# Sparse attention and a routed expert layer on one core: head pairs written in one hand order, with half-array scores, row copies by DMA and the last unit's sums on GpSimd

## The chip, the cores and the metric

The kernel runs on one core of a Trainium2 chip. A core has a TensorE (PE: matrix multiplications into PSUM), a VectorE (DVE), a ScalarE (ACT), a GpSimd (POOL, which also issues the indirect DMAs and the weight loads) and a SyncE (SP, which only issues DMAs). Each works through its own queue of instructions in order, and semaphores tie the queues together. The metric is the device time of one execution in microseconds (us); of several executions the median is compared.

## The reference

There are 4 batches of 8 heads, 768 tokens, 64 elements per head. Keys are cut into 24 chunks of 32. For each query an upper bound of its product with each chunk is computed from the chunk's minimum and maximum; the six best chunks that are not in the future are kept, and causal attention runs over those alone:

```python
ub = np.sum(np.maximum(q * k_min, q * k_max), axis=-1)   # per query and chunk
top_chunks = np.argsort(np.where(causal, ub, -1e9), axis=-1)[..., -6:]
scores = np.where(sel & (pos_q >= pos_k), (q @ k.T) / 8, -1e9)
x = softmax(scores) @ v                  # rows of 8 heads x 64 = 512
logits = x @ w_gate                      # 8 experts
out[token] = prob(best expert) * (relu(x @ w1[e]) @ w2[e])
```

The second part is a top-1 expert layer over the 3072 tokens: each token goes through one of 8 experts (512 to 1024 to 512) and is scaled by the gate's probability.

## The kernel before

**Head pairs.** Attention works on 16 pairs of heads, i = 0 to 15, four per batch (`hp` is the pair's place in its batch). For each pair, Q, K and V are loaded as 128 tokens by (6 blocks, 2 heads, 64). Several steps for different pairs run at the same time:

- *Preparation* (`prep_steps`, L191 to L268). TensorE turns K and Q by transposes (L202, L212), three 128-column blocks at a time. VectorE takes each chunk's maximum and minimum (L204, L205) and copies Q in f32 (`qT`, L219); ScalarE takes |Q| (`qA`, L220) and writes the bf16 operands: both heads' halves of K into `KTE` (L206, L207), the second head's half of Q into `QSB` (L222). GpSimd writes the first head's half of Q (L221). `kse` puts sums and differences of maxima and minima into `KS` and `KD` (L229, L230).
- *Selection*. `ub` multiplies `KS` with Q and `KD` with |Q| (L236), both heads and both halves of the queries in 64-row blocks; `select` turns the result (L244), adds a causal bias (L247), finds the eight largest per row (L252) and marks what lies below the sixth (L255). `mask` turns the marks (L262) and ScalarE writes them into rows 64 and up of `QSB` (L264, L265), where they meet rows of -50 in `KTE`, so that the score matmul adds the mask.
- *Attention*. Seven units u = 0 to 6 per pair: units 0 and 1 are the first 384 queries, 2 to 6 the second. `scores` is a bf16 matmul of 128 keys by up to 384 queries per head (L291), an exp on ScalarE (L296) into a tile `P`, and causal masks on GpSimd for the diagonal blocks (L300): units 0, 1 (twice), 5, 6 (twice). `attend` multiplies V with `P` in f32, each head on half of the array's columns (L313), copies the output when it is complete (`ot`, L318), and adds the unit's `P` to a running sum `acc` on VectorE (L325), which later gives the denominators.
- *Router* (`router_steps`, `route_steps`). `ud` takes denominators and gate products for the pair on 32-column pieces of the array (L341, L346); `lgp` turns them and divides (L354 to L358); `xr` turns the outputs, scales them and writes the token rows (L377, L379). Once per batch `logits`, `rank` and `scatter` choose experts and send the rows to DRAM in expert order.

**Order.** TensorE, GpSimd and SyncE follow the program's order. In the pairs, VectorE and ScalarE are ordered by the framework's planner; only the first pair and the last pair with the experts are by hand for them too. A pair is cut in four groups g (L722 to L771): units (0, 1), (2, 3), (4, 5), (6), and around them the steps of pairs i - 1, i + 1 and i + 2, with the scores 0 and 1 of pair i + 1 in the last group. Weights come in 32 pieces (`load_w`), spread over the groups on GpSimd's queue.

**Array shape.** A matmul uses the whole 128x128 array, or 64 or 32 of its columns, by the width of its stationary operand. Scores and transposes of f32 tiles use all of it; attend, `ub` and the mask's transposes 64; `ud` 32.

**Buffers.** PSUM has 8 banks: three in `ps_m` (preparation, selection, router), two of two banks each in `ps_s` (scores), one in `ps_o` (attend's output).

**Experts.** 28 tiles of 128 tokens are gathered (L542), turned by DMA (L554), and go through `up` (L589, Relu at L592, turned by DMA at L593) and `down` (L600, scaled at L607, scattered at L608).

Of the kernel before, what the change touches and what calls it, by code (L numbers as in the profile page):

```python
# [12 lines left out]
I32 = mybir.dt.int32  # L13
# [11 lines left out]
def kernel(  # L25
# [52 lines left out]
    cbias = const.tile([128, 3, 2, NCH], FP32)  # L78
    thr = const.tile([128, NT], FP32)
# [26 lines left out]
    def consts_first():  # L106
# [3 lines left out]
        colc = work.tile([128, S], BF16, tag="Pr", bufs=4, name="colc")  # L110
# [11 lines left out]
        nc.gpsimd.memset(nsel[:], 0.0)  # L122

    def consts_bias():
# [4 lines left out]
        for t in range(NT):  # L129
            nc.vector.tensor_scalar(thr[:, t:t + 1], chunk_p[:], float(4 * t), None, ALU.add)  # L130
# [4 lines left out]
    def consts_last():  # L135
        nc.gpsimd.memset(KS[1][:], 0.0)
        nc.gpsimd.memset(KD[1][:], 0.0)
        nc.gpsimd.memset(QSB[1][64:128], 0.0)
        nc.gpsimd.tensor_copy(out=KTE[1][64:128], in_=KTE[0][64:128])
# [18 lines left out]
    def load_w(s_):  # L158
# [7 lines left out]
        nc.gpsimd.dma_start(out=dst, in_=src.rearrange("(c p) f -> p c f", p=128))  # L166

    late, sums_ = [], []

    def flush(*qs):  # L170
        for q_ in qs or (sums_, late):
            for f_ in q_:
                f_()
            q_.clear()
# [5 lines left out]
    def load(i, *names, eng=nc.sync):  # L180
        b, hp = divmod(i, HP)
        for nm, src in (("k", k), ("q", q), ("v", v)):
            if nm not in names:
                continue
            t_ = ld.tile([128, NT, 2, D], FP32, tag=nm, bufs=2 if nm == "v" else 1)
            for hd in range(2):
                eng.dma_start(out=t_[:, :, hd, :],
                                  in_=src[b, 2 * hp + hd].rearrange("(t p) d -> p t d", p=128))
            st[i][nm] = t_

    def prep_steps(i):  # L191
        s = st[i]
        kte, qsb, ks, kd = KTE[i % 2], QSB[i % 2], KS[i % 2], KD[i % 2]
        kmx = {}

        def k_half(hf):
            if hf == 0:
                s["kmx"] = work.tile([128, NCH], FP32, tag="kmx", name="kmx")
                s["kmn"] = work.tile([128, NCH], FP32, tag="kmn", name="kmn")
            pt = ps_m.tile([128, 384], FP32, tag="m")  # L200
            for t in range(3):
                nc.tensor.transpose(pt[:, ts(t, 128)], s["k"][:, 3 * hf + t], ident_f[:])  # L202
            pk = pt[:].rearrange("p (c w) -> p c w", w=CH)
            nc.vector.tensor_reduce(s["kmx"][:, ts(hf, 12)], pk, AX.X, ALU.max)  # L204
            nc.vector.tensor_reduce(s["kmn"][:, ts(hf, 12)], pk, AX.X, ALU.min)  # L205
            nc.scalar.activation(kte[0:64, 0, ts(hf, 384)], pt[0:64, :], AF.Copy, bias=0.0, scale=0.125)  # L206
            nc.scalar.activation(kte[0:64, 1, ts(hf, 384)], pt[64:128, :], AF.Copy, bias=0.0, scale=0.125)  # L207

        def q_t(hf):
            pt = ps_m.tile([128, 384], FP32, tag="m")  # L210
            for t in range(3):
                nc.tensor.transpose(pt[:, ts(t, 128)], s["q"][:, 3 * hf + t], ident_f[:])  # L212
            s[f"qp{hf}"] = pt

        def q_e(hf):
            pt = s[f"qp{hf}"]
            qT = work.tile([128, 384], FP32, tag=f"qT{hf}")
            qA = work.tile([128, 384], FP32, tag=f"qA{hf}")
# [13 lines left out]
        def ub():  # L232
            pu = ps_m.tile([128, 384], FP32, tag="m")
            for w_, nm in ((ks, "qT"), (kd, "qA")):
                for hf in range(2):
                    nc.tensor.matmul(pu[64 * hf:64 * hf + 64, :], lhsT=w_[:], rhs=s[f"{nm}{hf}"][:],  # L236
                                     start=(nm == "qT"), stop=(nm == "qA"), skip_group_check=True)
# [626 lines left out]
```

## Time and profile before

| what | value |
|---|---|
| median of 3 runs | 364.26 us (364.17 to 366.05) |
| the profiled execution's own time | 363.95 us |
| its span, first to last instruction | 362.1 us |
| TensorE busy | 335.4 us, 93% |
| ScalarE busy | 235.2 us, 65% |
| VectorE busy | 232.1 us, 64% |
| GpSimd busy | 177.1 us, 49% |
| first scores | 16.7 us |
| denominators of pair 0, of pair 13 | 41.89 and 231.90 us |
| first `up`, last matmul of `down` | 248.8 and about 352.5 us |

All values but the first row come from one profiled execution. In a line of a group of instructions stand the source line, the engine, the operation, what is written and read, the shape, how often, then busy time and the mean duration of one; in a line of the timeline, the start, the length and the same names. For a matmul the words before the element shape are the array's rows and columns in use. An f32 matmul leaves two records. Matmuls overlap in the pipeline, so the distance between starts says more than a duration.

### The profile page before, as it was taken

To read this page: it belongs to the slowest core of one execution; us is meant where nothing else is said; L and a number is where in the kernel's file an instruction comes from. 1 tells how busy PE (TensorE), PEld (TensorE's weight loads), DVE (VectorE), ACT (ScalarE), POOL (GpSimd) and SP (SyncE) were. 2 spreads that over 40 slices of the span, in tenths; PEclk is the share of its full clock that TensorE was granted. 3 is DMA by queue.
4 is the path that set the end of the run, shared out by engine and by line. 5 is a ranking of instruction groups with operands and counts; after the bars stand their busy time and mean duration, and the time that the engine had idled before them with its cause. 6 is when DMAs were issued, how large, how long until landed. Compare 5 with 4: busy or idle time off the path is not lost. (4 is left out here: it accounts for less than half of the span.)

```text
span 362.1 us, 7547 instructions
## 1 busy us (share of the span) xinstructions
PE 335.4 (93%) x2312; PEld 173.4 (48%) x2312; DVE 232.1 (64%) x811; ACT 235.2 (65%) x398; POOL 177.1 (49%) x296
## 2 busy tenths in 40 slices
PE   6777999999999999999999997998999899999990
PEld 5534455465554554554545544443544344444440
DVE  5789788898998898998988999775370010000000
ACT  2496797797887977977879778462354445544450
POOL 3074333452476343457424538375576765555331
PEclk9999999999999999999999998999999999999996
DMA  7619997999948989957989992366999999999841
GB/s 148 114 24 198 201 206 113 217 194 177 219 108 185 191 121 195 205 123 193 167 138 201 183 186 67 83 125 121 164 193 236 204 245 211 215 197 193 175 123 51
DMA packets 138215, 59.83 MB, mean 165 GB/s; under 512 B 122811, under 2 KB 131005, under 8 KB 138176
## 3 DMA queue, kind: packets, MB, share of 16 engines
q1 hardware_dynamic: 119072, 29.52, 45.9%
q0 software_dynamic: 17536, 29.42, 42.0%
q10 hardware_dynamic: 1568, 0.39, 0.6%
q8 instruction: 21, 0.34, 0.4%
q14 instruction: 18, 0.15, 0.1%
HBM read 56.14 MB, written 10.51 MB: 184 GB/s over the span
## 5 line engine op out<-in xcount | busy, mean ns | idle before, releaser
L325 DVE TENSOR_TENSOR Pa<-Pa,Pr 128x768 f32<-128x768 f32 (+2 forms) x112 | 81.5, 728 | 1.8 <-DVE Pa L325 0.5
L300 POOL TENSOR_SCALAR_AFFINE_SELECT Pr<-Pr 128x256 f32<-128x256 f32 x80 | 31.9, 418 | 76.2 <-ACT Pr L296 75.3
L296 ACT ACTIVATE Pr<-ps 128x768 f32<-128x768 f32 (+2 forms) x112 | 65.0, 628 | 3.2 <-PE ps L291 2.9
L600 PE MATMUL py<-w_all,hT 128*128 x224 | 52.6, 379 | 1.0 <-DMA hT<-h__4066 0.8
L291 PE MATMUL ps<-QSB,KTE 128*128 128x384 bf16 (+2 forms) x288 | 49.1, 294 | 1.7 <-ACT QSB L265 1.2
L542 POOL DMA_INDIRECT xg<-xs_dram,grow x28 | 29.9, 1068 | 22.6 <-DVE gt_all L565 7.4
L563 DVE TENSOR_TENSOR ti_all<-xg,inv_i 128x1 int32<-128x1 int32 x17 | 2.8, 163 | 58.0 <-DMA xg<-xs_dram,grow 58.0
L291 PEld LDWEIGHTS <-KTE 128*128 128x128 bf16 x288 | 24.2, 98 | 32.6 <-issue 25.3
L608 POOL DMA_INDIRECT out_dram<-y,ti_all x28 | 27.8, 994 | 24.4 <-ACT y L607 18.7
L600 PEld LDWEIGHTS <-hT 128*128 128x128 bf16 x224 | 21.8, 98 | 27.6 <-DMA hT<-h__4066 1.2
L607 ACT ACTIVATE y<-py,gt_all 128x512 f32<-128x512 f32 x27 | 18.5, 687 | 20.6 <-PE py L600 19.9
L349 ACT ACTIVATE ud<-pu 128x384 f32<-128x384 f32 x16 | 7.9, 492 | 36.5 <-PE pu L346 36.5
L443 POOL DMA_INDIRECT xs_dram<-xrow,sli x24 | 26.9, 1121 | 6.6 <-issue 4.5
L589 PE MATMUL ph<-w_all,KTE 128*128 x120 | 28.4, 379 | 0.0
L296 ACT ACTIVATE Pa<-ps 128x768 f32<-128x768 f32 x32 | 26.0, 813 | 2.9 <-PE ps L291 2.3
L166 POOL DMA_DIRECT2D w_all<-in_moe_w_dram x32 | 24.4, 762 | 0.0
L300 POOL TENSOR_SCALAR_AFFINE_SELECT Pa<-Pa 128x256 f32<-128x256 f32 x16 | 6.5, 405 | 36.5 <-ACT Pa L296 36.5
L589 PE MATMUL ph<-w_all,QSB 128*128 x96 | 22.7, 379 | 0.2 <-issue 0.2
L379 DVE TENSOR_TENSOR xrow<-pt,rec 128x384 bf16<-128x384 f32 x32 | 17.6, 552 | 3.0 <-PE pu L236 1.7
L204 DVE TENSOR_REDUCE kmx<-pt 128x12 f32<-128x384 f32 x30 | 16.7, 556 | 4.0 <-PE pt L202 3.9
L221 POOL CAST QSB<-qT 64x384 bf16<-64x384 f32 x30 | 16.7, 564 | 4.1 <-DVE qT L219 2.7
L318 DVE COPY ot<-po 128x384 f32<-128x384 f32 x32 | 17.7, 553 | 1.2 <-PE po L313 1.2
(306 smaller groups left out, 639.5 us busy)
## 6 DMA issues: line engine op xcount, KB each, us to landing
w_all<-in_moe_w_dram POOLq DMA_DIRECT2D x32, 512.0 KB, 6.0
xg<-xs_dram,grow POOLq DMA_INDIRECT x28, 3.9
out_dram<-y,ti_all POOLq DMA_INDIRECT x28, 4.3
t__122<-in_k_dram SPq DMA_DIRECT2D x2, 192.0 KB, 3.5
t__125<-in_q_dram ACTq DMA_DIRECT2D x2, 192.0 KB, 4.0
t__128<-in_v_dram SPq DMA_DIRECT2D x2, 192.0 KB, 5.6
t__196<-in_k_dram SPq DMA_DIRECT2D x2, 192.0 KB
t__206<-in_q_dram SPq DMA_DIRECT2D x2, 192.0 KB, 3.7
```

Of the source, the lines that this page charges most:

```text
L166: nc.gpsimd.dma_start(out=dst, in_=src.rearrange("(c p) f -> p c f", p=128))
L291: nc.tensor.matmul(pv[:, hd, :], lhsT=kte[:, hd, ts(kb, 128)], rhs=qsb[:, hd, ds(qb * 384 + 384 - w, w)], start=True, stop=True, skip_grou ...
L296: nc.scalar.activation(P[:, :, ds(c0, w)], pv, AF.Exp)
L300: nc.gpsimd.affine_select(out=pd, in_=pd, pattern=[[0, 2], [1, 128]], compare_op=ALU.is_ge, fill=0.0, base=0, channel_multiplier=-1)
L318: nc.vector.tensor_copy(out=ot[:], in_=po[:])
L325: nc.vector.tensor_tensor(acc[:, :, 384 - w:384], acc[:, :, 384 - w:384], P[:, :, ds(c0, w)], ALU.add)
L443: d = nc.gpsimd.indirect_dma_start(out=xs_dram[:], out_offset=bass.IndirectOffsetOnAxis(ap=sli[:, u:u + 1], axis=0), in_=bst[b][f"xrow{u % ...
L542: d = nc.gpsimd.indirect_dma_start(out=xg_bufs[j % XB][:].bitcast(I32), out_offset=None, in_=xs_dram[:], in_offset=bass.IndirectOffsetOnAx ...
L589: nc.tensor.matmul(ph[:, fh, :], lhsT=xT[:, c, :], rhs=w_all[:, ds(wo + (c * F + fh * 512), 512)], start=(c == 0), stop=(c == NDC - 1), sk ...
L600: nc.tensor.matmul(py[:], lhsT=hT[:, c, :], rhs=w_all[:, ds(wo + (W1W + c * DM), DM)], start=(c == 0), stop=(c == NFC - 1))
L607: nc.scalar.activation(y[:], py[:], AF.Copy, bias=0.0, scale=fs[j]["gt"])
L608: d = nc.gpsimd.indirect_dma_start(out=out[:], out_offset=bass.IndirectOffsetOnAxis(ap=fs[j]["ti"], axis=0), in_=y[:], in_offset=None, bou ...
```

## The change

- **One order for all engines.** All five queues follow one written order, `iteration(i)`, for every pair; the planner orders nothing in the pairs any more. `prep_steps`, `scores` and `attend` are cut into smaller steps (matmul, evacuation, sum), so that each can be placed alone.
- **Two visits of the full array.** Within a pair, everything that needs all 128 columns stands in two places: Q's and the selection's transposes with scores 2 and 3; and scores 6 with K's, the gate's and the output's transposes. Scores 0, 1, 4 and 5 are computed as two halves of 64 keys each (`split=True`), on 64 columns of the array (not units 0 and 1 of pair 0).
- **Rows by DMA.** K and Q are written once in bf16 for both heads (`kB` by ScalarE, `qB` by GpSimd), and `rows` copies each head's 64 rows into `KTE` and `QSB` with two DMAs on SyncE.
- **Sums on GpSimd.** The two additions of unit 6 run on GpSimd behind that unit's masks. The second output of a pair is copied by ScalarE instead of VectorE.
- **Less of the first block.** The first 128 queries need no selection; the bounds, the bias and the mask cover 640 queries in 2 x 320 columns (`c0s`, `cbase`).
- **Exp in one piece.** Units 1 and 6 place their two parts side by side, and one exp covers both.
- **PSUM.** The output of the first half comes from `ps_m`, K's transposes from `ps_s`. `Pr` has three buffers instead of four.
- **First pair.** K and Q are loaded with one head on each of two queues, V later; the mask is computed twice into two banks, which ScalarE and VectorE empty at the same time.
- **Weights.** Half of the pieces (`w2`) are laid out so that a partition takes four rows in a row; Relu reads its PSUM tile with a stride so that `h` matches.
- **Router and table.** Logits stand early in a batch's second pair, and the early expert table is built in one piece in pair 14.

```diff
+    def k_red(i, hf):
+        pk = s["pk"][hf].rearrange("p (c w) -> p c w", w=CH)
+        for nm, op in (("kmx", ALU.max), ("kmn", ALU.min)):
+            d = nc.vector.tensor_reduce(s[nm][:, ts(hf, 12)], pk, AX.X, op)
...
+    def k_ev(i, hf):
+        d = nc.scalar.activation(st[i]["kB"][:, ts(hf, 384)], st[i]["pk"][hf], AF.Copy, bias=0.0, scale=0.125)
...
+    def rows(i, nm, dst):
+        for hd in range(2):
+            nc.sync.dma_start(out=dst[i % 2][0:64, hd, :], in_=st[i][nm][64 * hd:64 * hd + 64, :])
...
+    def q_c(i):
+        for hf in range(2):
+            nc.gpsimd.tensor_copy(out=st[i]["qB"][:, ts(hf, 384)], in_=st[i]["qT"][:, hf])
...
+                nc.tensor.matmul(pu[64 * h:64 * h + 64, 0:320], lhsT=w_[i % 2][:],
+                                 rhs=x_[:, ds(128 + 320 * h, 320)],
...
+    def s_mm(i, u, split=False):
+        for kb, w, c0 in parts:
+            for hd in range(2):
+                for h in range(2 if split else 1):
+                    n = 64 if split else 128
+                    nc.tensor.matmul(ps[ds(h * n, n), hd, ds(c0, w)], lhsT=kte[:, hd, ds(kb * 128 + h * n, n)],
+                                     rhs=qsb[:, hd, ds(qb * 384 + 384 - w, w)],
...
+    def add(i, u):
+        for kb, w, c0 in parts:
+            (nc.gpsimd if u == 6 else nc.vector).tensor_tensor(acc[:, :, 384 - w:384], acc[:, :, 384 - w:384], P[:, :, ds(c0, w)], ALU.add)
...
-            nc.scalar.activation(h_[:], ph[:], AF.Relu)
+            nc.scalar.activation(h_[:].rearrange("q a (c p) -> q a c p", c=4),
+                                 ph[:].rearrange("q a (p c) -> q a c p", c=4), AF.Relu)
...
+    def iteration(i):
+        p, n, m = i - 1, i + 1, i + 2
+        for u in (0, 1):
+            s_mm(i, u, i > 0)
+            s_ex(i, u)
+        if i > 1:
+            rout[i - 2]["sums"]()
...
+            av(p, 6)
+            if not last:
+                load(n, "v")
+            o_ev(p, 1)
+            if router:
+                route[b - 1][0]()
+            if n < NP:
+                ub_mm(n)
+                ub_ev(n)
+            if m < NP:
+                q_prep(m)
+            if n < NP:
+                sel_mm(n)
+                sel_v(n)
...
+        for u in (2, 3):
+            s_mm(i, u)
+            s_ex(i, u)
...
+        pieces(i, 2)
+        av(i, 0)
+        av(i, 1)
+        add(i, 1)
+        o_ev(i, 0)
...
+        for u in (4, 5):
+            s_mm(i, u, True)
+            s_ex(i, u)
+        if 0 < i and m < NP:
+            q_c(m)
+        pieces(i, 1)
...
+        av(i, 2)
+        av(i, 3)
+        add(i, 3)
+        add(i, 4)
...
+            mask_ev(n, mask_mm(n))
+        if i > 0:
+            rt["ud_mm"]()
+            rt["ud_ev"]()
+        s_mm(i, 6)
+        if m < NP:
+            rows(m, "qB", QSB)
+        s_ex(i, 6)
...
+        add(i, 5)
+        add(i, 6)
...
+        if m < NP:
+            k_prep(m, True)
+            rows(m, "kB", KTE)
+            kse(m)
+        if i > 0:
+            rt["lgp_mm"]()
+            rt["lgp_v"]()
...
+            av(i, 4)
+        av(i, 5)
```

## The prediction

> **What bounds the kernel now.** I read the page first: engine shares, then the 40 slices.
>
> ```profile
> span 362.1 us, 7547 instructions
> ...
> PE 335.4 (93%) x2312; PEld 173.4 (48%) x2312; DVE 232.1 (64%) x811; ACT 235.2 (65%) x398; POOL 177.1 (49%) x296
> ...
> PE   6777999999999999999999997998999899999990
> ...
> DVE  5789788898998898998988999775370010000000
> ```
>
> TensorE is busy from slice 5 to slice 39, so it looks like the bound of attention and of the experts; VectorE is close behind, but only in the attention slices. A busy share can hide waits, so next I asked for the engines' busy time in one head pair, and then for TensorE's order of time in the same stretch.
>
> ```profile
> 131.40:145.60 14.20, 14.12 (x110) 7.57 (x109) 12.59 (x39) 11.65 (x22) 6.15 (x14) 1.00 1.08 182
> ```
>
> (Columns: length; busy time of PE, PEld, DVE, ACT, POOL; clock; DMA share; GB/s.) The first matmul of the denominators (L341) comes back every 14.19 us, pair after pair, so 14.2 us is the pitch.
>
> ```profile
> 133.40 0.82 PE L212 MATMUL pt<-ident_f,t__1831 128*128 128x128 f32 x6
> 134.15 0.87 PE L313 MATMUL po<-Pr,t__1683 128*64 128x256 f32 x8
> 134.95 0.82 PE L291 MATMUL ps<-QSB,KTE 128*128 128x384 bf16 x4
> ...
> 136.24 0.87 PE L313 MATMUL po<-Pa,t__1888 128*64 128x384 f32 x4
> 136.93 0.82 PE L313 MATMUL po<-Pr,t__1888 128*64 128x256 f32 x8
> 137.58 0.81 PE L236 MATMUL pu<-qT,KS 128*64 128x384 f32 x4
> 138.23 0.81 PE L236 MATMUL pu<-qA,KD 128*64 128x384 f32 x4
> 138.97 0.85 PE L291 MATMUL ps<-QSB,KTE 128*128 128x384 bf16 x4
> 139.72 0.55 PE L244 MATMUL pt<-ident_f,ubT 128*128 128x128 f32 x3
> 140.20 0.87 PE L313 MATMUL po<-Pa,t__1888 128*64 128x384 f32 x4
> 140.89 0.81 PE L313 MATMUL po<-Pr,t__1888 128*64 128x384 f32 x4
> 141.64 0.85 PE L341 MATMUL pu<-Pa,dcol 128*32 128x384 f32 x8
> ```
>
> Two things are to be seen. The fourth word from the end is the array shape: 128*128, 128*64 or 128*32. It changes nine times per pair. The same eight records of L313 (256 and 128 columns) take 0.65 us between two groups of their own shape (136.93 to 137.58), and 0.80 between two groups of full shape (134.15 to 134.95); the six transposes ahead of it, 0.109 apart, need 0.65 and the next group starts after 0.75. So a change of shape costs 0.10 to 0.15 us on the engine that sets the pitch. Single records show more: 0.24 us before L377, 0.14 before L377 again and 0.08 around L244 are waits. The pitch is thus 13.74 us of work and changes, and 0.46 of waits. After the pairs, a pair of L589 and L600 groups comes every 3.45 us, 16 matmuls of 0.216: the experts are TensorE's alone.
>
> **What the Trainium skill says.** *TensorEngine Tiling (Array Packing)*, Key Properties: changing the tiling mode, not just the tile, drains TensorE. The trace agrees: 0.202 us between starts at a change, 0.109 without. Its Restrictions say that column tiling disables fast weight load. The six bf16 transposes of L262, each with a 64-column load, start 0.056 us apart, so such loads hide here. *SBUF — State Buffer*, Who interferes with whom: a VectorE instruction with two SBUF inputs and a GpSimd instruction that reads SBUF exclude each other. The trace agrees:
>
> ```profile
> 136.69 0.48 DVE L229 TENSOR_TENSOR KS<-kmx,kmn 64x24 f32<-64x24 f32 x1
> ```
>
> The same instruction took 0.17 at 136.41; this one stood beside a cast on POOL (136.62 to 137.13) and ended with it.
>
> **The change, part by part, per pair.**
>
> *TensorE.* After the change its order is: scores 0, 1 as halves; unit 6 of the last pair; bounds; | Q turns, selection turns, scores 2, 3; | attend 0, 1; scores 4, 5 as halves; attend 2, 3; mask turns; | denominators and gates (32 columns); | scores 6, K turns, and the last pair's gate and output turns; | attend 4, 5. Five changes. From the group pitches above, with a change added only at a bar: 0.70 (halves: eight 0.163-equivalents, plus 0.05 for two loads per 0.056 stream) + 0.63 + bounds 1.16 (four streams of 0.32 cut from 384 to 320 columns, and a change) + 0.71 + 0.33 + 0.75 + 1.33 + 0.65 + 1.27 + 0.44 + 1.43 + 0.34 + 0.66 + 0.33 + 0.75 + 1.32 = 12.80 us, against 13.74. Halves are not shown in bf16; the f32 pairs of L313 start 0.006 apart and share 0.317. Bounds: nothing, or each half alone, which is 1.31 more (a rival). I take nothing.
>
> *ScalarE.* Before, by mean durations: exps 5 x 0.81 + 2 x (0.59 + 0.39) = 6.0, K 4 x 0.486, Q 4 x 0.488, masks 2 x 0.80, L349 and L239 0.98: 12.5. After: 7 x 0.81, K and Q 2 each, masks 2 x 0.67, 0.49 + 0.42, and the new copy of one output 0.49: 10.4. Not the bound, but strictly in order now.
>
> *VectorE.* It loses the unit-6 sums (starts 0.60 and 0.40 apart) and one output copy (0.47): 12.59 becomes 11.1.
>
> *GpSimd.* Casts keep their 384 columns on 128 instead of 64 partitions: 0.50 each if time goes by columns, as it seems to for L300 (128 partitions, 256 columns, 0.40); at worst double, +1.0, hidden. Two f32 sums are new. *GPSIMD Engine Reference*, Elementwise: 2.6 cycles an element at 1.2 GHz, 2.17 ns; with 0.18 fixed (the 48-element sum of L369 took 0.287) an estimate of 1.29 + 0.74 = 2.0 us. 6.15 becomes 8.2 of 13. Behind them on POOL stand the next pair's masks of units 0 and 1, wanted 5 us later. Their lock is dearer: add 5 on VectorE can meet the casts, and the K sums (KS, KD) the new adds. KS is wanted by the bounds matmul 1.3 us into the next pair.
>
> *Row copies by DMA.* Four of 96 KB per pair on SP, behind the loads of Q and K. The Q rows wait for the casts and scores 6; the K load is queued behind them, issued about 10 us into the pair, and K's turns come 12 us later, while such loads land in 3.5 to 5.6 us. The rows themselves are used a whole pair later. Nothing; if a row landed over 12 us late, all of the excess. They replace four half-width copies, counted above.
>
> *Waits.* By hand along the order: the second scores need the K bank, read by four reduces (0.465 apart) that begin only after add 5: ready within 0.3 us of need. The bounds need KS and the gate bank: 0 to 0.5 late. I take 0.40, near today's 0.46: pitch 13.2 us. VectorE's 11.1 plus up to 2 of lock stays just inside.
>
> *Router steps* (pairs 5, 9, 13). Logits now stand first on VectorE and wait for GpSimd's sums behind three masks, about 3.6 us in; ScalarE's exp of the logits waits for them ahead of the bounds copy, so selection turns come at 5.0 instead of 3.2, and Q's bank is freed late for attend 0. I take 2.0 us each (0.4 to 3). Step 14 has the early table in one piece on VectorE: 19 instructions of about 0.2, 3.8 us, against its missing K and Q work: 3.0 lost; before, that step lost 3.6 too.
>
> *Start.* K halves on two queues and V after them: TensorE waits 1.87 us for K; 0 to 1.5 less, I take 0.7. Two mask banks are emptied side by side (0.58 between the first two scores goes), six more transposes (0.34), four fewer spins (0.22): 0.4. Step 0 moves a lot but is VectorE's, some 14 us as now: 0, plus or minus 1.
>
> *Experts.* Same matmuls. Relu reads PSUM with a stride: ScalarE has 3.45 - 1.03 - 0.69 = 1.7 us spare per tile; 0 to 1.2 at the end; I take 0. One h buffer fewer waits for nothing: the slot's last reader is three tiles back. Half of the weight pieces come in longer runs: 0 or better, hidden, as no wait of TensorE on weights is listed.
>
> *Sum.* The denominators of pairs 0 and 13 are 190.0 us apart now. After: 13 x 13.2 + 3 x 2.0 + 3.0 = 180.6. Minus 9.4, minus 1.1 at the start: span 351.6. The profiled run took 363.95, 1.85 over its span, and the median is 0.3 above that: 353.7 us.
>
> **Rivals.** *Waits vanish* (pitch 12.9, router steps 1.0): 13 x 12.9 + 3 + 3 = 173.7; 347 us. For it: ScalarE and VectorE have spare time. Against: hand order lets nothing slip past a late one. *The lock becomes the bound*: VectorE 11.1 plus 2 to 3 us held by casts, masks and sums gives 14.0: 13 x 14.0 + 9 = 191; 364. For it: KS stretched once to 1.34 us. Against: 0.4 us of it per pair today. *Halves do not run side by side*, the slower side: each of ten half pairs doubles, +1.31, pitch 14.4 with 0.3 of waits: 13 x 14.4 + 4.5 + 3 = 194.7, and 1.3 in the last pair; 369 us. It decides from about 0.09 us a half pair on, half of 0.163. Against: f32 halves share. For: nothing shows two bf16 streams at once. *An order wait that I don't see*, over 1 us each pair: 363 to 371.
>
> **How the numbers follow.** Forecast 0.45 (own range 349 to 359), no waits 0.20 (343 to 349), lock 0.12 (360 to 366), halves 0.12 (366 to 373), order wait 0.11. Under 343 lies 0.03, over 368 some 0.14. A change under 0.5% (362.4 to 366.1) can't be told from none. Faster: 0.45 + 0.20 + 0.06 = 0.71; same 0.07; slower 0.22.
>
> **What would show it.** Right: five shape changes, L341 every 13.2 us, half-score pairs starting 0.006 apart and 0.163 per pair, POOL sums of 1.3 and 0.7. Wrong: half scores in single file; KS of 1 us and more; TensorE waiting for the K bank or the selection over 0.5 us in every pair, or for a row DMA at all.

## The result and the profile after

The changed kernel is slower: 384.74 us median (380.81 to 385.49) beside 364.22 for the kernel before on the same chip, a ratio of 1.054 with a 95% interval of 1.047 to 1.061. The forecast was 353.7 us. The profiled execution took 380.81 us and is the fastest of the five on record: the other four took 384.5 to 385.5 at a mean clock of 0.960 to 0.968, beside its 0.982, so some 4 of the 20.5 us between the medians are not in this trace.

The page of the changed kernel, the same lines as shown of before:

```profile
span 379.1 us, 7833 instructions
...
PE 327.3 (86%) x2458; PEld 188.3 (50%) x2468; DVE 224.8 (59%) x763; ACT 206.7 (55%) x322; POOL 222.5 (59%) x328
...
PE   7795989888896899987879979759889999999994
...
DVE  6577589896995968986769899583347000000000
```

TensorE has 8 us less to do and the span is 17 us longer: the row of TensorE, nines from slice 5 on before, now has sevens and eights among them all through attention. The work did shrink; the engine waits. Where the 17.0 us are is read from the starts of the denominators (L368, L341 before):

| stretch | before | after | forecast |
|---|---|---|---|
| start to pair 0 | 41.89 | 47.14 | 40.8 |
| pair 0 to pair 13 | 190.01 | 200.04 | 180.6 |
| pair 13 to the end of the span | 130.2 | 131.9 | 130.2 |

One step between pairs, and the wait at its head and at its tail, in the windows and in TensorE's order of time:

```profile
117.00:133.40 16.40, 13.37 (x120) 8.28 (x122) 11.79 (x36) 9.79 (x16) 11.36 (x17) 1.00 0.84 185
```

```profile
116.88 0.87 PE L337 MATMUL po<-P,v_t 128*64 128x256 f32 x8 [2.07 <-POOL P L323]
...
123.13 0.85 PE L306 MATMUL ps<-QSB,KTE 128*64 128x384 bf16 x8
123.78 1.49 PE L337 MATMUL po<-P,v_t 128*64 128x384 f32 x8
...
130.42 0.82 PE L306 MATMUL ps<-QSB,KTE 128*64 128x384 bf16 x12
133.29 0.87 PE L337 MATMUL po<-P,v_t 128*64 128x256 f32 x8 [2.04 <-POOL P L323]
```

TensorE has 13.4 us of work in the window of 16.4 (this pair has router work as well). Scores 4 and 5, eight half streams, take 0.65 us from start to start (123.13 to 123.78): halves share the array, 0.163 a pair of them, as the sum had it. Between scores 1 and the attend of unit 6 stand 2 us of waiting for a mask on GpSimd. From pair 0 to pair 13 TensorE has 26.6 us of recorded waits, and 20.3 of them are of two kinds: this one, and one for VectorE's divided logits (`lgt`), whose PSUM bank the bounds matmul needs (over the whole run; engine, what waits, what it waits for: total us, times, longest):

```profile
PE po L337 <- POOL P L323: 10.7, 6, 2.1
PE pu L250 <- DVE lgt L392: 10.0, 8, 1.7
```

Both begin on GpSimd. Its order of time in a pair of the second kind, and VectorE's beside it:

```profile
62.53 0.59 POOL L323 TENSOR_SCALAR_AFFINE_SELECT P<-P 128x256 f32<-128x256 f32 x1 [5.71 <-ACT P L319]
63.09 2.40 POOL L242 CAST qB<-qT 128x384 bf16<-128x384 f32 x2
65.43 0.56 POOL L168 DMA_DIRECT2D w_all<-in_moe_w_dram  x1
66.01 0.77 POOL L323 TENSOR_SCALAR_AFFINE_SELECT P<-P 128x256 f32<-128x256 f32 x2
66.74 2.07 POOL L345 TENSOR_TENSOR P<-P 128x512 f32<-128x512 f32 x2
```

```profile
67.02 1.04 DVE L222 TENSOR_TENSOR KS<-kmx,kmn 64x24 f32<-64x24 f32 x1
...
68.17 0.69 DVE L222 TENSOR_TENSOR KS<-kmx,kmn 64x24 f32<-64x24 f32 x1
...
69.25 0.26 DVE L392 TENSOR_TENSOR lgt<-pt,rec 128x96 f32<-128x96 f32 x1
```

The two casts take 2.40 us instead of 1.0. They stand where VectorE runs sums 3 to 5. The mask of unit 6 and its sums come behind them; the sums (66.74 to 68.81) then cover VectorE's K sums: the first KS takes 1.04 us, the second 0.69 and ends with GpSimd's sum, against 0.17 alone. `lgt` follows them in the queue, and the bounds of the next pair wait for it at 69.66. The page has the sizes:

```profile
L242 POOL CAST qB<-qT 128x384 bf16<-128x384 f32 x30 | 34.3, 1168 | 6.3 <-DVE qT L234 6.3
...
L345 POOL TENSOR_TENSOR P<-P 128x512 f32<-128x512 f32 (+1 forms) x32 | 32.0, 1000 | 1.3
```

A cast has a mean of 1.17 us (0.50 at the least, 1.22 in nearly every pair); the sums are what was estimated, 1.27 and 0.73 for the two forms. In a pair with a scatter, its three issues of 1.0 to 1.1 us stand between the casts and the mask, and the wait is the first kind.

**Theory A** from this trace: the hand order puts GpSimd's casts, masks and sums in one strict queue ahead of what TensorE wants next, and stretched casts make it late. **Rivals**: the strict order of VectorE and ScalarE costs as much wherever things stand (theory B); or the halves or the row copies cost more than they save (theory C). The first eight experiments were run where the kernel before took 371.8 us, so ratios and steps from pair to pair are compared, not times. In the experiments a step is the time from one pair's denominators to the next pair's, and "plain" pairs or steps are those without router or scatter work.

### The profile page after: what moved, and what is told of

It reads as the page before. It is cut to its first block, busy times and chain, and to the rows that moved or that the text cites. A ratio compares the mean times of both kernels' runs of the same rounds, so it can differ in the third digit from the quotient of the medians.

```text
span 379.1 us, 7833 instructions
## 1 busy us (share of the span) xinstructions
PE 327.3 (86%) x2458; PEld 188.3 (50%) x2468; DVE 224.8 (59%) x763; ACT 206.7 (55%) x322; POOL 222.5 (59%) x328
## 3 DMA queue, kind: packets, MB, share of 16 engines
q0 software_dynamic: 11392, 29.42, 36.6%
## 5 line engine op out<-in xcount | busy, mean ns | idle before, releaser
L319 ACT ACTIVATE P<-ps 128x768 f32<-128x768 f32 x112 | 87.3, 813 | 41.2 <-PE ps L306 29.0
L337 PE MATMUL po<-P,v_t 128*64 128x384 f32 (+2 forms) x576 | 87.8, 428 | 11.2 <-POOL P L323 10.7
L323 POOL TENSOR_SCALAR_AFFINE_SELECT P<-P 128x256 f32<-128x256 f32 x96 | 40.8, 448 | 89.1 <-ACT P L319 88.7
L345 DVE TENSOR_TENSOR P<-P 128x768 f32<-128x768 f32 (+2 forms) x80 | 65.7, 821 | 13.3 <-PE po L337 5.8
L337 PEld LDWEIGHTS po<-P,v_t 128*64 128x64 f32 x576 | 40.2, 139 | 41.3 <-issue 16.2
L306 PE MATMUL ps<-QSB,KTE 128*128 128x384 bf16 (+3 forms) x442 | 49.4, 298 | 1.3 <-ACT P L319 1.3
L306 PEld LDWEIGHTS <-KTE 128*128 128x128 bf16 (+1 forms) x442 | 31.5, 108 | 22.7 <-issue 17.8
L242 POOL CAST qB<-qT 128x384 bf16<-128x384 f32 x30 | 34.3, 1168 | 6.3 <-DVE qT L234 6.3
L345 POOL TENSOR_TENSOR P<-P 128x512 f32<-128x512 f32 (+1 forms) x32 | 32.0, 1000 | 1.3
L644 ACT ACTIVATE y<-py,gt_all 128x512 f32<-128x512 f32 x27 | 18.5, 687 | 19.5 <-PE py L637 18.9
L234 DVE COPY qT<-pq 128x384 f32<-128x384 f32 x30 | 16.2, 555 | 20.5 <-PE pq L185 17.2
L415 DVE TENSOR_TENSOR xrow<-px,rec 128x384 bf16<-128x384 f32 x32 | 16.6, 550 | 10.9 <-DMA xs_dram<-xrow,sli 10.7
```

The source lines that it names most:

```text
L242: nc.gpsimd.tensor_copy(out=st[i]["qB"][:, ts(hf, 384)], in_=st[i]["qT"][:, hf])
L306: nc.tensor.matmul(ps[ds(h * n, n), hd, ds(c0, w)], lhsT=kte[:, hd, ds(kb * 128 + h * n, n)], rhs=qsb[:, hd, ds(qb * 384 + 384 - w, w)], s ...
L319: nc.scalar.activation(P[:], ps[:, :, 0:384], AF.Exp)
L323: nc.gpsimd.affine_select(out=pd, in_=pd, pattern=[[0, 2], [1, 128]], compare_op=ALU.is_ge, fill=0.0, base=0, channel_multiplier=-1)
L337: nc.tensor.matmul(po[64 * hd:64 * hd + 64, 384 - w:384], lhsT=vt[:, kb, hd, :], rhs=P[:, hd, ds(c0, w)], start=first, stop=last and n == ...
L345: (nc.gpsimd if u == 6 else nc.vector).tensor_tensor(acc[:, :, 384 - w:384], acc[:, :, 384 - w:384], P[:, :, ds(c0, w)], ALU.add)
```

## Experiments

**1. The sums of unit 6 back on VectorE.**

```diff
-            (nc.gpsimd if u == 6 else nc.vector).tensor_tensor(...)
+            nc.vector.tensor_tensor(...)
```

> The changed kernel, with the two additions of unit 6 on VectorE again. Theory A (GpSimd's queue and the read port that it shares with VectorE set the pitch: KS waits for the sums on GpSimd, and the mask of unit 6 stands behind the Q casts): the wait of the bounds matmul for lgt (10.0 us in 8 pairs) falls below 4 us, the wait of unit 6's attend for its mask (10.7 us in 6) stays over 8; about 378 us against 384.7. Theory B (the strict hand order of VectorE and ScalarE is to blame, VectorE too full): 1 us more on VectorE in every pair makes it slower, 390 us or more. Theory C (half-array scores or row DMAs): no change, 383 to 386.

Measured: 431.25 us, ratio 1.163 (1.155 to 1.170). A miss for A; B, with 390 us or more, had the direction. The steps are 15.5 to 21.6 us.

```profile
PE ps L306 <- DVE kmn L202: 49.4, 14, 5.8
```

The sum now waits at the head of VectorE's queue for GpSimd's late mask; K's reduces stand behind it, they hold the bank of the next scores, and the scores wait up to 5.8 us. In a written order an instruction that is moved takes everything behind it along. The clock adds to it: some 74 us of this run lie in stretches at half clock.

**2. The casts on ScalarE, at their place. 4. That, and the unit-6 sums behind the next pair's first masks.**

```diff
-            nc.gpsimd.tensor_copy(out=st[i]["qB"][:, ts(hf, 384)], in_=st[i]["qT"][:, hf])
+            nc.scalar.activation(st[i]["qB"][:, ts(hf, 384)], st[i]["qT"][:, hf], AF.Copy)
# and in experiment 4
+        if i > 0:
+            add(p, 6)                      # behind s_ex(i, 1)
-        add(i, 6)
```

> The changed kernel, with Q's bf16 copies on ScalarE (from the same tile, at the same place in the order) in place of GpSimd. Theory A: 2.4 us go from GpSimd ahead of the mask of unit 6, so the attend of unit 6 waits under 3 us in all for it (10.7 now), the sums start 2 us earlier and KS is held less; pitch 13.2 to 13.6 us instead of 15.4, about 362 us (358 to 370). Theory B: two more copies of 0.49 on ScalarE push its masks and exps back, 384 us or more. Theory C: no change, 383 to 386.

> As the run with the casts on ScalarE, and the sums of unit 6 stand behind the next pair's masks of unit 1 on GpSimd, where VectorE reads PSUM. Theory A: KS takes 0.2 us again, the bounds wait for lgt is gone (under 1 us in all), pitch 13.0 to 13.3; about 358 us (354 to 364), so faster than the kernel before. Theory B: as without the move, within 1%.

Measured: 389.04 us, 1.043 (1.035 to 1.051), and 391.12 us, 1.054 (1.047 to 1.061): both far from what A expected. Taking the casts away frees the masks, but VectorE's K sums still meet the sums (0.63 and 0.70 us), and the casts, in ScalarE's queue ahead of `ud`, make the turns of the gate wait 0.7 us; plain steps 14.4. In experiment 4 KS is back at 0.17 us and the wait for `lgt` is gone, plain steps 13.8 to 13.9; but the steps with logits become 17.7 to 19.7, as the logits wait for their sums on GpSimd and block VectorE, and three early steps wait for the load of Q (5.4 us together).

**3. Scores whole.**

```diff
-            s_mm(i, u, i > 0)      # units 0, 1
+            s_mm(i, u)
-            s_mm(i, u, True)       # units 4, 5
+            s_mm(i, u)
```

> The changed kernel, with all scores on the whole array (no halves): four more changes of shape in a pair. Theory A: TensorE gains 0.5 to 0.6 us of work per pair, part of which falls into its waits for GpSimd: 0 to 8 us slower, 385 to 392. Theory C (halves don't share the array, or their loads cost): faster by 5 us or more, under 380.

Measured: 387.05 us, 1.045 (1.035 to 1.054), not to be told from the changed kernel. So C is out for the halves: they bring nothing while other queues set the pace, and cost nothing that shows.

**5. The order of the queues. 6. The ends too. 7. Experiment 6 with whole scores.** Experiment 5 is experiment 4 with Q's casts behind K's copies on ScalarE, the router's sums and logits at the end of the batch's first pair, and the scatter ahead of scores 4. Experiment 6 also moves the first selection, some constants, the table of pair 14, and lengthens the warm-up.

```diff
-        if 0 < i and m < NP:
-            q_c(m)                         # behind scores 5
+            if i > 0:
+                q_c(m)                     # behind k_prep(m)
+            rows(m, "qB", QSB)
...
+            rt["sums"]()                   # behind lgp_v
+            if hp == 0:
+                route[b - 1][0]()
# experiment 6
-            consts_last()
-            sel_mm(1)
-            sel_v(1)
+        if i == 0:
+            sel_mm(1)                      # behind scores 5 of pair 0
+            sel_v(1)
```

> As the run with casts on ScalarE and late sums, with three things moved in the order: the Q casts stand behind K's copies on ScalarE (where it idled 1.6 us) and no longer ahead of the masks; the router sums and logits stand at the end of a batch's first pair, where VectorE idled 1.4 us; the scatter stands ahead of scores 4. Theory A (single places in the five queues hold the pairs, and TensorE's 12.9 us floor is real): plain pairs 13.1 to 13.4 us instead of 13.8, router pairs under 15 instead of 18 to 20, ratio to before 0.98 to 1.01. Theory B (a strict order can't keep VectorE and ScalarE fed, whatever stands where): the waits move elsewhere, ratio 1.04 or more.

> As e5_order, and the ends: in pair 0 the selection for pair 1 goes ahead of sums 3 and 4 on VectorE and the constants behind the pair (TensorE waited 4.0 us for the marks there); 42 instead of 30 warming matmuls at the start (its first transposes ran at half clock); the early table behind sum 4 of pair 14 (TensorE waited 4.1 us there). Theory A: 6 to 10 us off e5_order, ratio 0.955 to 0.985. Theory B: under 4 us off.

> As e6_order_ends, without halves: all scores on the whole array, nine changes of shape per pair. Theory A, where TensorE sets the pitch: four changes at 0.15 us more in each of 14 pairs, 6 to 9 us slower than e6_order_ends. If the waits still set it: under 3 us slower. If halves cost: faster.

Measured: 386.44 us, 1.038 (1.033 to 1.043); 388.52 us, 1.044 (1.035 to 1.052); 385.65 us, 1.037 (1.029 to 1.045). The totals say that nothing helped; the steps say otherwise. Plain steps are now 12.84 to 13.15 us, the forecast's pitch, and others 13.7 to 19.5. The windows of two neighbours in experiment 6:

```profile
48.70:61.70 13.00, 12.98 (x124) 8.23 (x122) 11.21 (x37) 10.52 (x19) 6.67 (x12) 1.00 1.16 210
61.70:80.80 19.10, 14.46 (x119) 8.95 (x118) 11.96 (x36) 10.94 (x19) 6.85 (x14) 0.91 1.09 212
```

In the first TensorE is busy throughout; the DMA share, before the GB/s, is over 1 in both. What TensorE waits for most is new:

```profile
PE pq L185 <- DMA q_t<-in_q_dram: 15.4, 7, 4.6
```

So once the queues are in order, the load of Q is late. Either the sixteen DMA engines are full (theory D), or Q's load stands too far back in SyncE's strict queue, behind row copies that wait for scores (theory O). In experiment 7 the whole scores lengthen plain steps to 13.4 to 14.0, and the wait for Q goes from 15.4 to 13.2 us.

**8. The changed kernel with the router's moves alone.**

```diff
-            rout[i - 2]["sums"]()          # ahead of av(p, 6)
+            rt["sums"]()                   # behind lgp_v
```

> The changed kernel, with only the router sums, logits and scatter moved as in e5_order (casts and unit-6 sums stay on GpSimd at their places). Theory A: the masks of unit 6 no longer stand behind three scatters, so the waits of 2.3 us of unit 6's attend (5 pairs) go, and logits no longer hold Q; the bounds' waits for lgt stay: 8 to 12 us off, ratio 1.02 to 1.035. Theory B: ratio 1.05.

Measured: 385.60 us, 1.039 (1.033 to 1.046). The wait of attend 6 is gone, that for `lgt` stays (11.8 us), as A had it; the ratio lies between what A (1.02 to 1.035) and B (1.05) expected, as new waits for the reduces of K (5.7 us) take a part back.

**9. Experiment 6 with the weights asked for evenly.**

```diff
-    npiece = [3, 3, 3, 3, 3, 0, 2, 2, 2, 0, 2, 2, 3, 0, 2, 2]
+    npiece = [1, 2, 2, 2, 2, 2, 2, 2, 2, 2, 2, 2, 2, 2, 2, 3]
-        pieces(-1, 2)
```

> The reordered kernel of experiment 6, with the expert weights asked for evenly: two pieces in each of pairs 1 to 14, one in pair 0, three in pair 15 and none ahead of pair 0, in place of three in pairs 0 to 4 and 12 and none in pairs 5, 9 and 13. The order of every queue and the row copies stay. Theory D (the sixteen DMA engines are full where a pair asks for three pieces): such a pair moves six loads of 192 KB, four row copies of 96 KB and three pieces of 512 KB, 3.15 MB, which at the 205 to 212 GB/s that experiment 6 shows there is 15 us, over a pitch of 13; with two pieces it is 2.6 MB or 12.5 us. So the waits of Q's transposes for their load (12.9 us in experiment 6, at pairs 2, 4, 10 and 12) fall under 4 us and the clock stays up: 370 to 377 us beside the 371.8 of before, ratio 0.995 to 1.015. Theory O (Q's load is late because it stands behind the row copies, and those behind the scores, in SyncE's queue of strict order): nothing of that is changed, the waits stay, 384 to 390, ratio 1.03 to 1.05.

Measured: 375.07 us, 1.032 (1.024 to 1.039); the kernel before took 365.3 on this chip. The ratio lies where O had it. The steps show what it hides: pair 0 to pair 14 takes 200.0 us against 209.1 in experiment 6, and the waits for Q's load fall from 15.4 to 7.5 us with SyncE's order untouched, as D has it and O does not, though D had under 4. The three pieces given to pair 15 take some of it back: the last step goes from 9.4 to 13.5 us.

**10. Experiment 6, and 11. experiment 9, without the row copies**, one head's K written by VectorE.

```diff
+            d = nc.vector.tensor_scalar(KTE[i % 2][0:64, 1, ts(hf, 384)], pk[64:128], 0.125, None, ALU.mult)
-            rows(m, "kB", KTE)
-            rows(m, "qB", QSB)
```

> The kernel of experiment 6 without the row copies of pairs 2 to 15: ScalarE and VectorE write K's rows, and ScalarE Q's rows, straight to their place, one head at a time (ScalarE two copies of 64 partitions more, about 1.0 us a pair, VectorE two more, about 0.9). Both theories expect fewer waits for Q's load. Theory D: a pair with three pieces still needs 2.75 MB, 13.1 us at 210 GB/s, just at the pitch, so some 2 to 5 us of the 12.9 are left: 374 to 381 us, ratio 1.005 to 1.025. Theory O: with nothing in SyncE's queue that waits for scores the loads start in time and the waits vanish whole: 369 to 374. Third (ScalarE and VectorE, now near 12.5 us each, set the pitch): plain pairs go to 13.5 to 14, 380 or more.

> Experiments 9 and 10 together, and the routing table of the last pair but one in three parts as in the kernel before (its last part behind the turns that need the buffer which it shares). Theory D: 2.2 MB a pair, 10.6 us, so no pair waits for a load; plain pairs 12.9 to 13.3, router pairs 13.5 to 15, and the wait of 3.8 us at step 14 gone: 362 to 370 us, ratio 0.975 to 0.995, the first of these to beat the kernel before. If ScalarE's two more copies set the pitch: plain pairs 13.5 or more and 370 to 378.

Measured: 412.01 us, 1.126 (1.120 to 1.132), and 412.11 us, 1.127 (1.119 to 1.135). Both miss what D and O expected, and tell nothing of the row copies: the edit made a wait of its own.

```profile
ACT KTE L217 <- DVE KTE L213: 51.3, 27, 3.5
```

ScalarE's copy waits for VectorE's copy out of the same bank into the same tile. Experiment 18 does it without this.

**12. Experiment 9 with the next late thing in each queue moved. 13. The scatter taken apart, and the start.** Experiment 12 puts V's load behind Q's, the scatter behind masks or router sums, the exponentials of the logits behind the next selection, the table in three parts, no weights in pair 15. Experiment 13 splits the scatter into single issues, writes half of one pair's x rows a pair later, and turns Q of pair 2 at the end of pair 0.

```diff
# experiment 12
-    npiece = [1, 2, 2, 2, 2, 2, 2, 2, 2, 2, 2, 2, 2, 2, 2, 3]
+    npiece = [1, 2, 2, 2, 2, 2, 2, 2, 2, 2, 2, 2, 2, 3, 4, 0]
             if m < NP:
                 q_prep(m)
+            if not last:
+                load(n, "v")
...
+        if router:
+            route[b - 1][3]()              # exp of the logits, behind sel_v(n)
# experiment 13
+    npiece = [1, 2, 2, 2, 2, 2, 2, 3, 2, 2, 2, 3, 2, 2, 3, 0]
```

> Experiment 9 with what its trace shows as the next place in each queue moved on: V's load behind Q's in SyncE's queue; the scatter of the router behind GpSimd's mask of unit 5 (first half) and behind the sums of the router (second half); the exponentials of the logits, which ScalarE held at the head of its queue for 2.0 us, behind the next pair's selection; the routing table in three parts, its last behind the turns that share a buffer with it; no weights in pair 15 (three pieces in pair 13, four in pair 14). The theory that the change lowers TensorE's need to 12.9 us a pair and that only the order of the other queues and the even use of the DMA engines kept it from the clock: plain pairs 12.9 to 13.3 us, the six router pairs 13.3 to 14.2 (14.9 to 15.2 in experiment 9), step 14 at 11.3, step 15 near 8.5; from the start of pair 0's sums to pair 13's 172 to 178 us (190.0 before, 186.1 in experiment 9); ratio to the kernel before 0.955 to 0.985. The rival that the row copies and the cut streams cost the other engines what they save TensorE whatever the order: pairs stay at 14 to 15 and the ratio at 1.01 to 1.03.

> Experiment 12 with the scatter taken apart: in the batch's second pair one of its six issues behind GpSimd's mask of unit 5 and two behind the mask of unit 6, in the third pair two ahead of the mask of unit 5 and one behind it; weights in those pairs at their end; the second half of the x rows of the batch's first pair written one pair later, so that VectorE does not wait for a scatter at the head of its queue (2.8 and 1.7 us in experiment 12); the ranks behind the output copy; Q of pair 2 at the end of pair 0 (its load landed 2.5 us after TensorE asked for it). Theory of order: router pairs 13.0 to 14.0 us (14.2 to 18.9 in experiment 12), step 14 at 11.0 to 11.8, pair 0 1.5 to 3 us earlier; from pair 0 to pair 13 169 to 175 us (188.9 there); ratio to the kernel before 0.955 to 0.980. Rival (a price of the change that no order takes away): other waits of the same size take their place, pair 0 to 13 stays over 182, ratio over 0.995.

Measured: 368.65 us, 1.010 (1.006 to 1.015), and 373.46 us, 1.029 (1.024 to 1.034). Experiment 12 has plain steps of 12.98 to 13.65 and loses the rest at the scatter, whose 3.7 us of issues stand ahead of masks (8.3 us of waits). Experiment 13 takes most of that away and pair 0 comes 3.4 us earlier, yet it is slower, and by accident it is the sharpest test of D. Its weights had three pieces in pairs 7 and 11 and two around them. The two steps that follow, 13.65 us each in experiment 12, take 20.51 and 18.61; the first of them:

```profile
136.72 1.09 PE L185 MATMUL pq<-ident_f,q_t 128*128 128x128 f32 x4 [4.96 <-DMA q_t<-in_q_dram]
```

```profile
124.10:144.60 20.50, 15.53 (x120) 9.25 (x118) 12.20 (x37) 11.14 (x19) 6.52 (x14) 0.83 1.13 217
```

The DMA engines move 217 GB/s and their share is 1.13 through the whole step. By the sizes of the transfers a plain pair with three pieces moves 6 x 0.197 + 4 x 0.098 + 3 x 0.524 = 3.15 MB, an estimated 14.5 us at that rate, over the pitch of 13; with two it is 2.6 MB, 12.1 us. The wait is 5 us; the step lost 6.9, since the clock is at half for 6.8 us from 135.0 on. The Trainium skill, *TensorE: Matmul & The Clock Gate*, Part 1, says that the clock falls to half after at least one idle window of about 3.4 us. The stretches at half clock in these traces are 3.4 and 6.8 us long, which agrees with the window's length. Less idleness than a whole window was enough, though: in experiment 14 the clock fell at 146.37 behind a single wait of 2.03 us, while five waits of 2.04 to 2.09 us in the changed kernel's profile left it at full.

**14. Experiment 13 with at most two pieces where K and Q are loaded. 15. Experiment 14 with the casts back on GpSimd, at their place of the changed kernel. 16. Experiment 14 with whole scores.**

```diff
# 14
+    npiece = [1, 2, 2, 2, 2, 2, 2, 2, 2, 2, 2, 2, 2, 5, 2, 0]
# 15
-            nc.scalar.activation(st[i]["qB"][:, ts(hf, 384)], st[i]["qT"][:, hf], AF.Copy)
+            nc.gpsimd.tensor_copy(out=st[i]["qB"][:, ts(hf, 384)], in_=st[i]["qT"][:, hf])
# 16
-            s_mm(i, u, True)
+            s_mm(i, u)
```

> Experiment 13 with no pair that loads K and Q given more than two pieces of weights (five in pair 13 and two in pair 14, which load neither), and the pieces of the router's pairs asked for where GpSimd is idle. Theory of order and even use of the DMA engines: pairs 7 and 11 from 20.5 and 18.6 us to 13.0 to 13.6; router pairs 13.5 to 15.5 as in experiment 13 (VectorE has some 14 us of work there); pair 0 to 13 at 178 to 183 us (197.2 there, 190.0 before); about 354 to 358 us, ratio to the kernel before 0.970 to 0.988. Rival (a price that no order takes away): ratio over 0.995.

> Experiment 14 with one thing put back: Q's two casts a pair on GpSimd, behind its mask of unit 5 as in the changed kernel, in place of ScalarE. If the casts, stretched beside VectorE's sums, are the step that failed: they take 1.0 to 1.2 us each in place of 0.5, the mask of unit 6 and the sums behind it come 2 us later, pairs go from 13.0 to 13.8 to 14.6, and the run is 12 to 20 us over experiment 14. If the casts hurt only together with the other parts: 0 to 4 us over it.

> Experiment 14 with one thing put back: scores of units 0, 1, 4 and 5 whole, as in the kernel before, and not in halves of 64 keys that share the array. In the sum of the prediction the halves are worth 1.31 us a pair (four units at 0.163 us a stream of 384 twice); where TensorE sets the pitch the plain pairs go from 13.0 to 14.0 to 14.3 and the run is 11 to 17 us over experiment 14, back at the time of the kernel before. If the other engines set it: 0 to 5 us over it.

Measured beside the same runs of the kernel before (364.42 us): 363.44 us, 0.998 (0.996 to 1.000); 366.51 us, 1.007 (1.004 to 1.010); 363.04 us, 0.996 (0.993 to 0.998). Experiment 14 missed its 0.970 to 0.988: the steps behind pairs 7 and 11 are short again (13.13 and 13.92), but one other step has 2.0 us of waiting for Q and the clock at half behind it (17.43), and behind the five pieces of pair 13 TensorE waits 1.4 and 3.1 us for V's load, in a step of 21.8.

The casts put back cost 3.1 us in all, not 12 to 20:

```profile
L242 POOL CAST qB<-qT 128x384 bf16<-128x384 f32 x30 | 28.5, 976 | 10.3 <-DMA QSB<-qB 5.8
```

They are still stretched to 0.98 us, and plain steps stay at 12.9 to 13.1 up to pair 3: with the sums out of the way the lateness has no victim. So A was half right: a stretched cast costs much only with the sums and K's reduces behind it. How the loss divides between casts, sums and scatter is not shown, since no run moves the sums alone.

Whole scores cost nothing in the total, and my expectation of 11 to 17 us was badly made: the 1.31 us a pair of the prediction is the price of halves in single file, not of whole scores, whose 384 columns take the same 0.163 us as two halves side by side. What they do cost is shape changes:

```profile
56.00:69.40 13.40, 13.38 (x112) 7.75 (x108) 11.17 (x35) 10.46 (x19) 6.22 (x13) 1.00 1.04 191
```

TensorE is busy all of a plain pair at a pitch of 13.44, against 12.99 with halves: 0.45 us for four changes of shape, 0.11 each, as read before. In pairs bound by other queues or by transfers this is not seen.

**17. Experiment 14 with three and four pieces in pairs 13 and 14. 18. That without row copies**, ScalarE writing both heads.

```diff
# 17
+    npiece = [1, 2, 2, 2, 2, 2, 2, 2, 2, 2, 2, 2, 2, 3, 4, 0]
# 18
-            outs = [(st[i]["kB"][:, ts(hf, 384)], pk)]
+            outs = [(KTE[i % 2][0:64, hd, ts(hf, 384)], pk[64 * hd:64 * hd + 64]) for hd in range(2)]
...
-            rows(m, "kB", KTE)
-            rows(m, "qB", QSB)
```

> Experiment 14 with three pieces of weights in pair 13 and four in pair 14, in place of five and two. Theory of the DMA engines: the step from pair 12 to 13, 21.8 us with 5.3 us of waits for V's load and the clock at half behind them, falls to 14.5 to 15.5; pair 14 with four pieces and one load of V carries 2.5 MB and stays within its 12 us or lengthens by up to 2; in all 4 to 7 us under experiment 14, ratio to the kernel before 0.978 to 0.990. If pair 14 takes the late transfer in its place: ratio 0.990 to 1.000.

> Experiment 17 without the row copies of pairs 2 to 15: ScalarE writes K's and Q's rows straight to their place, two copies of 64 partitions each in place of one of 128, so four instructions or about 2.0 us a pair more on ScalarE (10.5 to 12.5 busy in 13.0), and 0.39 MB a pair less to move of 2.6. If the row copies load the DMA engines so that loads of Q come late: the waits for Q's load (3.4 us in experiment 14) vanish and router pairs shorten by up to 1 us, 3 to 6 us under experiment 17. If ScalarE's 12.5 us in a queue of strict order cost more: plain pairs 13.3 to 14.2, 4 to 14 us over experiment 17.

Measured: 358.64 us, **0.987 (0.983 to 0.991)**, the fastest of all (only experiment 16 is under the kernel before too, by 0.4%); and 366.15 us, 1.005 (1.002 to 1.007). The windows of two plain steps of experiment 17, from denominators to denominators:

```profile
53.92:66.91 12.99, 12.98 (x121) 8.23 (x119) 11.20 (x37) 10.51 (x19) 6.22 (x12) 1.00 1.07 197
66.91:79.91 13.00, 12.97 (x120) 8.22 (x118) 11.19 (x37) 10.51 (x19) 6.20 (x12) 1.00 0.89 177
```

TensorE is full, VectorE has 11.2 of 13 us and ScalarE 10.5. Pair 0 to pair 13 takes 181.65 us, beside the forecast's 180.6. Without the row copies plain steps are 13.98 us and no wait for Q's load is left, but one of 0.9 us in a plain pair, and more in others, takes its place:

```profile
PE pt L275 <- ACT ubT L268: 15.7, 14, 2.0
```

ScalarE's four more copies come at the end of the pair, ahead of the next pair's exps and of the bounds' copy, so the selection turns wait. The row copies are thus worth about 1 us a pair, as long as the DMA engines have room for them. Two things still separate experiment 17 from its plain pitch: steps with logits, ranks and x rows are 13.7 to 14.8 us, where VectorE's reduces of K and GpSimd's sums of unit 6 come late (2.8 and 2.9 us of waits), and the last pairs. Whether the halves bring anything in this version is open: it was not run with whole scores.

## Why the prediction was wrong, by its own steps

- **TensorE, 12.80 us: right within 0.2.** The shortest step of the changed kernel is 13.90 us with one wait, which takes 0.87 (1.52 from start to start where 0.65 is usual), so about 13.0; experiment 17 shows 12.98 to 13.01. Halves share (0.163 a pair, though they start 0.036 apart and not 0.006), the bounds lost their columns, the shape changes cost 0.11 each.
- **GpSimd: the step that failed first.** "0.50 each if time goes by columns ... at worst double, +1.0, hidden": a cast took 1.17 us in the mean, 0.50 only where VectorE left it alone, and it was not hidden. The text warned that "add 5 on VectorE can meet the casts", and priced it as VectorE's loss. The exclusion works both ways, and beside a long run of sums on VectorE it is GpSimd that waits. The sums were right (1.27 + 0.73 against 1.29 + 0.74).
- **"Behind them on POOL stand the next pair's masks of units 0 and 1, wanted 5 us later": the wrong neighbour.** That looks behind the sums alone. What stands behind the casts is unit 6's own mask, wanted by the attend at the head of the next pair, and in scatter pairs three issues of 1.1 us come between. The sums behind that mask then block KS.
- **Waits, 0.40 a pair: the term that carries the miss.** The two kinds alone are 20.3 us within the 13 steps, where the forecast had 5.2 us of waits beside its router terms. That is some 15 of the 19.4 us between 180.6 and 200.04. "0 to 0.5 late" was counted on queues without stretched instructions.
- **Row copies, "Nothing": right for the changed kernel, wrong below it.** TensorE never waits for a row. But, as the Trainium skill says (*DMA: Bandwidth & Descriptors*, Issuing engines are not separate DMA queues), DMAs of all queues run on the same sixteen engines; experiment 13 agrees, where one more piece of weights on GpSimd's queue makes a load on SyncE's queue 5.0 us late. There 0.39 MB of rows a pair leaves no room for three pieces of weights in 13 us. I had not added up the transfers of a pair: with three pieces they are an estimated 14.5 us at 217 GB/s, next to TensorE's 13.0.
- **Router steps 2.0 each, step 14 3.0: not the place of the loss.** In the changed kernel steps with and without router work are 13.9 to 16.7, for the mask and bank waits above; in experiment 17, where these two kinds are nearly gone, logits and ranks lengthen a step by 1.5 to 1.8 us.
- **Start, minus 1.1, step 0 unchanged: wrong.** Pair 0 came 5.25 us later. The first scores come at 17.53 us instead of 16.73; TensorE reaches full clock at 10.2 us (5.1 before) and falls to half again for 3.4 us behind a wait of 2.2 for the first marks. Then the mask of pair 1 waits 3.5 us for VectorE's marks, which stand behind other work in the written order, and scores 1 of pair 1 wait 1.1 more for a bank that ScalarE empties late; from 34.1 us on the clock is at half for 6.8 us. With the order of experiment 17 the start is at 40.93 us, 0.96 earlier than before.
- **Experts, 0: right by luck.** The last stretch of the table is 1.7 us longer, but three parts hide in it. From pair 13 to the first `up` it is 23.0 us instead of 16.9, as the last pairs wait too (3.9 us for `ud` alone). The experts themselves, first `up` to last `down`, are as forecast: 102.9 and 103.3. From there to the end it is 6.0 instead of 10.0, a gain that nobody forecast. In every profile of the changed kernel and its variants this tail is 6.0 to 6.5 us. The closing drain of GpSimd is 3.2 us shorter (the longest of three, in ns, before and after):

```profile
L859 POOLq DRAIN  x3: 51/103/5215, 356.1 to 361.9; - x3
```

```profile
L945 POOLq DRAIN  x3: 51/103/2056, 376.2 to 378.8; - x3
```

Its DMA queue has 11,392 packets instead of 17,536, as half of the weight pieces come in longer runs. That this is the reason is likely and not shown; no run changes it alone.
- **The rivals.** "The lock becomes the bound" (364 us) and "an order wait" (363 to 371) named the right two things and gave them 0.23 together; they came together, and each was priced for one place in each pair.

What is shown: with only the order of the queues, the engine of the casts, the times of the weight loads and the length of the warm-up changed, the same arithmetic and row copies take 0.987 of the time of the kernel before. From pair 0 to pair 13 it went from 200.0 us to 192.3 (experiment 5), 186.1 (9) and 181.7 (17), beside 190.0 before. The span in the profile of experiment 17 is 7.0 us shorter than before: these pairs give 8.4 of it, the start 1.0 and the tail 4.0, and 6.4 are lost again between pair 13 and the last `down`. Without the tail, which may have nothing to do with the order, some 3 us would be left. What stays open: how the 6.3 us that separate the start from its forecast split between order and clock, and why TensorE's wait for Q differs by 2 us between runs of the same order (experiments 14 and 17).

## What to carry to other kernels

When a planner's order is replaced by a written one, count for each engine not its work but its queue: what stands behind every instruction that can be late or stretched, and who waits for that. Adding up the work of the engine that bounds gives only the floor, and a second sum belongs beside it, the bytes that one period moves over the DMA engines' rate. Mend one place at a time and read the steps, not the total: the changed kernel and experiments 2 to 8 had the same ratio within 2% while their shortest steps went from 13.9 to 12.9 us.

## What the hardware showed unexpectedly

- Two casts of 128x384 on GpSimd go from 0.50 to 1.2 us beside VectorE's sums of two SBUF tiles; a 64x24 sum on VectorE goes from 0.17 to 1.04 beside a GpSimd sum.
- One wait of 5 us cost the step 6.9 us, as TensorE then ran at half clock for 6.8 us; elsewhere a single wait of 2.03 us was enough for the clock to fall.
- Issues on SyncE are not always short: in experiment 6 the two issues of a load took 5.9 and 6.1 us at 64.30 and 75.92, in a step with a DMA share of 1.09, and 0.96 at 83.43. That full DMA engines stretch them is likely, and not shown.
